# Linear attention into a gated MLP, batch 0: k loaded ahead of q, beta under the loads, kv evacuated from two banks by DVE and ACT

## The chip, the cores and the metric

One Trainium2 chip, one of its cores. The metric is the device time of one launch in microseconds (us); several runs are taken and the median is quoted. A profile is one execution; its span (first to last instruction) is some 2 us shorter than the time of the same run (300.0 against 301.74 us in the kernel before). TensorE (PE), VectorE (DVE), ScalarE (ACT) and GpSimd (POOL) run side by side (busy for 287.4, 123.9, 176.1 and 52.0 of the 300.0 us of the kernel before); POOL issues nearly all of the loads here, into one queue (q0 of the page, 20.45 MB, 47.1% of the time of 16 DMA engines); only beta's 8 KB go by SyncE.

## The reference, cut to what matters

```python
batch, n_heads, seq, head_dim = (8, 8, 576, 64)
phi = lambda x: np.where(x > 0, x, np.exp(x) - 1.0) + 1.0
q_p, k_p = (phi(q), phi(k))
kv  = np.einsum('bhsd,bhse->bhde', k_p, v)
z   = np.sum(k_p, axis=2)
num = np.einsum('bhsd,bhde->bhse', q_p, kv)
den = np.einsum('bhsd,bhd->bhs', q_p, z)[..., None] + 1e-06
x   = (num / den)            # 4608 tokens x 512
h   = x @ w_in               # 512 x 2048
g   = h * (1.0 / (1.0 + np.exp(-beta * h)))
out = g @ w_out              # 2048 x 512
```

## The kernel before

Batches run in a pipeline: the attention of batch b+1 is done under the h and y matmuls of batch b (y is g @ w_out). Batch 0 has nothing to hide under, so its loads and its attention are the start of the program. It uses a layout of nine tokens per partition: partitions 0 to 63 hold heads 0 to 3 (g = 0), partitions 64 to 127 heads 4 to 7 (g = 1).

```python
    load_nine(q9, q, j1=4)          # the queue's order: q's first 4 of 9 tokens
    load_nine(k9, k)
    make_identity(nc, identity)
    make_identity(nc, ident16)
    load_nine(v9, v, h1=2)
    load_nine(v9, v, h0=2)
    load_nine(q9, q, j0=4)
    for i in range(4):
        nc.gpsimd.dma_start(out=w_in_sb[i], in_=w_in_v[:, :, i * 512 : (i + 1) * 512])
    load_w_out(0)
    load_w_out(1)
    load_k(1)                       # k and q of batch 1
    load_q(1)
    # ... cut ...
    warm(WARM)                      # 20 matmuls on zeros
    beta_trans()
    # ... cut ...
    exp0(0, 0, 4)                   # 0 is q, 1 is k
    relu0(0, 0, 4)
    phi0(0, 0, 4)
    exp0(1, 0, 5)
    exp0(1, 5, N9)
    qb = att_banks(BF16)
    q_trans0(0, qb, 0)
    q_trans0(1, qb, 256)
    warm(8)
    q_out0(0, qb, 0, False)
    q_out0(1, qb, 256, False)
    relu0(1, 0, 5)
    relu0(1, 5, N9)
    phi0(1, 0, 5)
    phi0(1, 5, N9)
    v_copy0(0, 2)
    make_beta()                     # five small DVE operations
    kvp = att_banks()               # one tile of two banks
    kv_mm0(0, kvp)                  # 18 matmuls
    warm(2)
    v_copy0(2, HH)
    kv_mm0(1, kvp)                  # 18 matmuls
    kv_evac0(kvp)                   # two DVE copies of 64 x 260
    warm(3)
    num_mm(0, 0)
    num_mm(0, 1)
    # ... cut: exp of q's rest, table load for Silu, num_norm, x_trans, then h_phase(0) ...
    h_last(0, xT[0], [F(exp_, 1, 1), F(exp_, 1, 0), F(w_out_scale, 2, dve=False)])
```

`warm` is there to keep TensorE's clock from falling (before_warm and kq1_less_warm below test it: with more of these matmuls the granted clock from 12.3 to 15.7 us was 1.00 for 0.51, with fewer 0.51 for 1.00). `h_last` is the end of batch 0's h phase; the exps of batch 1's k and q follow it on ACT.

## Time and profile before

| | before |
|---|---|
| median of 4 runs (301.73 to 302.92) | 302.12 us |
| profiled span | 300.0 us |
| exp of k starts | 10.12 us |
| first h matmul of batch 0 | 20.73 us |
| ACT's table load for the exps of batch 1 | 35.69 us |

### The profile page before, as it was taken

What the parts mean: (1) busy time and instruction counts of PE and PEld (TensorE: products, weight loads), DVE (VectorE), ACT (ScalarE), POOL (GpSimd) and SP (SyncE); (2) the same over time, 40 slices, a digit from 0 to 9 for tenths busy, and PEclk for the clock granted to TensorE, in tenths of its full rate; (3) what the DMA queues carried; (4) which work ended last, traced back from release to release, by engine and by line L of the source; (5) the groups of instructions that cost most, each with busy time, mean ns of one, the idle gap of its engine ahead of it and who ended that gap; (6) DMA issues with size and microseconds to landing.
All of it is one profiled execution on the core that took longest, in us unless ns stands there. A gap on an engine that the chain in (4) does not pass through costs nothing.

```text
span 300.0 us, 4706 instructions
## 1 busy us (share of the span) xinstructions
PE 287.4 (96%) x1877; PEld 146.1 (49%) x1898; DVE 123.9 (41%) x248; ACT 176.1 (59%) x232; POOL 52.0 (17%) x72
## 2 busy tenths in 40 slices
PE   8599998999999999999999999999999999999994
PEld 3257545654556444445444544454445444444444
DVE  4567495801476145714571457144714400110012
ACT  3448896789988791579157915691661067007600
POOL 8834466432202300060002000000000000000000
PEclk9879999999999999999999999999999999999999
DMA  6999999999917974399538165125412510010033
GB/s 80 195 207 341 248 278 192 213 234 181 161 40 192 164 124 123 97 155 173 129 94 111 53 98 130 29 56 130 98 26 57 127 37 0 35 72 35 0 71 71
DMA packets 69206, 36.43 MB, mean 121 GB/s; under 512 B 37808, under 2 KB 63680, under 8 KB 69184
## 3 DMA queue, kind: packets, MB, share of 16 engines
q0 software_dynamic: 38400, 20.45, 47.1%
q1 hardware_dynamic: 30624, 15.55, 20.5%
q8 instruction: 15, 0.25, 0.3%
q10 hardware_dynamic: 160, 0.13, 0.2%
q14 instruction: 7, 0.06, 0.1%
HBM read 36.71 MB, written 9.44 MB: 154 GB/s over the span
## 4 chain that ended last, share of the span: by engine, by line
PE 81%; ACT 7%; DMA 4%; issue 3%; DVE 2%; POOL 1%; ACTq 0%; POOLq 0%
PE mm L443 39%; PE mm L495 33%; PE att L389 3%; ACT e L225 3%; DMA xqk<-in_k_dram 2%; DMA xqk<-in_q_dram 2%; PE att L335 2%; PE mm L527 1%; PE mm L562 1%; ACT q_pT L362 1%; ACT w_out L210 1%; ACT L225 1%; PE att L301 1%; ACT e L252 1%; POOL xqk L133 1%
## 5 line engine op out<-in xcount | busy, mean ns | idle before, releaser
L435 ACT ACTIVATE g<-mm,beta_c 128x512 bf16<-128x512 f32 (+2 forms) x156 | 97.4, 632 | 92.3 <-PE mm L443 91.9
L495 PE MATMUL mm<-w_out,g 128*128 128x512 bf16 x541 | 127.4, 379 | 1.2 <-issue 0.3
L443 PE MATMUL mm<-xT,w_in 128*128 128x512 bf16 (+2 forms) x560 | 107.8, 349 | 0.8 <-DVE xT L360 0.8
L443 PEld LDWEIGHTS <-w_in 128*128 128x128 bf16 x656 | 62.2, 98 | 61.7 <-issue 1.0
L495 PEld LDWEIGHTS <-g 128*128 128x128 bf16 x560 | 52.7, 97 | 57.1
L505 DVE COPY y_sb<-mm 128x512 f32<-128x512 f32 x27 | 18.7, 692 | 70.4 <-PE mm L495 68.4
L225 ACT ACTIVATE e<-xqk 128x2560 bf16<-128x2560 bf16 x14 | 31.9, 2329 | 0.1
L405 DVE TENSOR_TENSOR xs<-att,rden 128x512 bf16<-128x512 f32 (+1 forms) x40 | 27.6, 690 | 1.6 <-DVE rden L404 0.2
L238 DVE TENSOR_TENSOR qk_p<-r,e 128x2560 bf16<-128x2560 bf16 x14 | 20.9, 1490 | 14.6 <-ACT e L225 13.9
L345 DVE CAST kv_bd<-att 64x260 bf16<-64x260 f32 x14 | 6.0, 427 | 36.8 <-PE att L335 36.7
L73 POOL DMA_DIRECT2D vraw<-in_v_dram x7 | 6.2, 881 | 77.0 <-DVE vaug L360 71.0
L403 DVE TENSOR_SCALAR den<-att 128x8 f32<-128x8 f32 (+1 forms) x40 | 6.5, 161 | 29.1 <-PE att L389 29.1
L389 PEld LDWEIGHTS <-q_pT 128*128 128x128 bf16 (+1 forms) x160 | 12.2, 103 | 10.9 <-DVE xs L405 2.1
L389 PE MATMUL att<-kv_bd,q_pT 128*128 128x130 bf16 (+1 forms) x160 | 16.4, 227 | 0.8 <-ACT q_pT L362 0.5
L443 PE MATMUL mm<-xT_tail,w_in 128*128 128x512 bf16 x63 | 13.9, 379 | 0.1
L233 DVE TENSOR_SCALAR r<-xqk 128x2560 bf16<-128x2560 bf16 x14 | 11.6, 836 | 4.4 <-DMA xqk<-in_q_dram 2.2
L562 PE MATMUL mm<-g 128*128 128x512 bf16 x36 | 11.8, 483 | 1.6 <-DVE g L145 1.2
L73 POOL DMA_DIRECT2D xqk<-in_k_dram x7 | 7.0, 1005 | 15.6 <-ACT e L225 8.5
L252 ACT ACTIVATE e<-xqk 128x1024 bf16<-128x1024 bf16 (+1 forms) x4 | 4.5, 1159 | 8.2 <-DMA xqk<-in_q_dram 4.3
L225 ACT ACT_TABLE_LOAD x7 | 9.0, 1283 | 0.1
L73 POOL DMA_DIRECT2D xqk<-in_q_dram x7 | 7.7, 1102 | 5.9 <-DMA w_in<-in_moe_w_in_dram 1.9
L404 DVE RECIPROCAL rden<-den 128x8 f32<-128x8 f32 (+1 forms) x40 | 8.1, 201 | 1.4
(72 smaller groups left out, 144.9 us busy)
## 6 DMA issues: line engine op xcount, KB each, us to landing
out_dram<-y_sb SPq DMA_DIRECT2D x28, 256.0 KB, 2.3
xqk<-in_k_dram POOLq DMA_DIRECT2D x7, 512.0 KB, 10.7
xqk<-in_q_dram POOLq DMA_DIRECT2D x7, 512.0 KB, 11.6
vraw<-in_v_dram POOLq DMA_DIRECT2D x7, 512.0 KB, 12.3
w_in<-in_moe_w_in_dram POOLq DMA_DIRECT2D x4, 512.0 KB, 10.2
g<-in_moe_w_out_dram POOLq DMA_DIRECT2D x4, 512.0 KB, 11.1
out_dram<-y_sb SPq DMA_DIRECT2D x14, 128.0 KB, 5.2
xqk<-in_moe_w_out_dram POOLq DMA_DIRECT2D x2, 512.0 KB, 13.9
```

The source lines that it names most:

```text
L73: eng.dma_start(out=dst[:, :, 0:NJ, :].rearrange("p h j d -> p h (j d)"), in_=src[b, :, 0:MAIN, :].rearrange("h (p j) d -> p h (j d)", j=NJ),)
L225: nc.scalar.activation(st[b, "e", a][:, h0:h1], xqk[b % NX][:, a, h0:h1], ACTF.Exp)
L233: nc.vector.tensor_scalar(st[b, "r", a][:, h0:h1], xqk[b % NX][:, a, h0:h1], 0.0, 1.0, ALU.max, ALU.add)
L238: nc.vector.tensor_tensor(st[b, "p"][:, a].rearrange("p j (h d) -> p h j d", h=H)[:, h0:h1], st[b, "r", a][:, h0:h1], st[b, "e", a][:, h0: ...
L389: nc.tensor.matmul(nps[:n, p // 2, c0 : c0 + 2 * (D + 1)], st[b, "qT"][:, t, p, :n], kv_bd[b % 2][:, p], start=True, stop=True, skip_group ...
L404: nc.vector.reciprocal(rden[:n], den[:n])
L405: nc.vector.tensor_mul(xs[:n], nv[:, :, :, 0:D], rden[:n, :, :, None].to_broadcast([n, 2, 4, D]))
L435: nc.scalar.activation(g_sb[b % 2][:, ff, c0:c1], hp[:, c0:c1], ACTF.Silu, scale=beta_c[:, ff : ff + 1],)
L443: nc.tensor.matmul(hp[:, c0:c1], w_in_sb[ff // 4][:, kc, (ff % 4) * P : (ff % 4 + 1) * P], x[:, t0:t1, kc, :] if b < B else x[:, kc, c0:c1 ...
L495: nc.tensor.matmul(yp, g_sb[b % 2][:, ff, t * P : (t + 1) * P], w_out_sb[ff // 4][:, ff % 4, :], start=(ff == 0), stop=(ff == FC - 1),)
L505: nc.vector.tensor_copy(y_sb, yp)
L562: nc.tensor.matmul(st["warm"], g_sb[0][:, FC - 1, 0:P], g_sb[0][:, FC - 1, :], start=True, stop=True, skip_group_check=True,)
```

## The change

Its intent: k is needed before q, so it is loaded first; beta needs only DVE and a small transpose, so it is done while the loads run; the two head halves, which already lie in two banks of one tile, get a tile each, and the evacuation is split by bank, so that DVE empties one while ACT empties the other. The core of the diff:

```diff
+    load_nine(k9, k)
     load_nine(q9, q, j1=4)
-    load_nine(k9, k)
@@ kv_evac0, kv_bd split in two tiles by head half g
-        for i in range(2):
-            copy(kv_bd[0][gs, :, i, :]..., kvp[gs, :, ...], True)
+        for g in range(2):
+            for i in range(2):
+                copy(kv_bd[0][g][gs, :, i, :], kvp[g][gs, ...], g == 0)
@@ the start of batch 0 (cut)
-    warm(WARM)
+    warm(10)
     beta_trans()
-    exp0(0, 0, 4)  relu0(0, 0, 4)  phi0(0, 0, 4)
-    exp0(1, 0, 5)  exp0(1, 5, N9)
+    make_beta()
+    warm(20)
+    exp0(1, 0, 5)  exp0(1, 5, N9)  exp0(0, 0, 4)
+    relu0(1, 0, 5) relu0(1, 5, N9) phi0(1, 0, 5)
+    relu0(0, 0, 4) phi0(1, 5, N9)  phi0(0, 0, 4)
+    v_copy0(0, 2)
     q_trans0(0, qb, 0)
     q_trans0(1, qb, 256)
-    warm(8)
+    kvp = [mm_bank([P, 512]) for _ in range(2)]
+    kv_mm0(0, kvp)
     q_out0(0, qb, 0, False)
     q_out0(1, qb, 256, False)
-    # ... k's relu and phi, v_copy0(0, 2), make_beta, kv_mm0(0), warm(2) ...
+    warm(1)
     v_copy0(2, HH)
     kv_mm0(1, kvp)
     kv_evac0(kvp)
-    warm(3)
+    warm(1)
@@ plan of the h phase
-            3: [F(x_trans, 0, 1, dve=True), ...
+            3: [F(x_trans, 0, 1), ...
```

Because kv_bd is split, the later batches evacuate kv with four DVE copies of 64 x 130 in place of two of 64 x 260.

More of the change, by code (lines that the diff above doesn't have):

```diff
@@ L41 @@
     DMA_T = 3
-    WARM = 20
     TINY = 2.0 ** -30
@@ L165 @@
     load_q(1)
-    kv_bd = [consts.tile([P, KC, 2, D + 1], BF16, name=f"kv_bd{i}") for i in range(2)]
+    kv_bd = [
+        [consts.tile([P, 2, 2, D + 1], BF16, name=f"kv_bd{i}{g}") for g in range(2)]
+        for i in range(2)
+    ]
     for i in range(2):
-        nc.vector.memset(kv_bd[i], 0.0)
+        for g in range(2):
+            nc.vector.memset(kv_bd[i][g], 0.0)
     def set_ones(i):
@@ L301, in kv_mm0 @@
                 nc.tensor.matmul(
-                    kvp[:, g, m0 : m0 + 2 * (D + 1)],
+                    kvp[g][:, m0 : m0 + 2 * (D + 1)],
                     st["p0"][1][gs, j, 2 * a : 2 * a + 2, :],
@@ L308, in kv_evac0 @@
     def kv_evac0(kvp):
-        for i in range(2):
-            gs = slice(i * D, (i + 1) * D)
-            copy(
-                kv_bd[0][gs, :, i, :].rearrange("p (g a) e -> p g a e", g=2),
-                kvp[gs, :, 0 : 4 * (D + 1)].rearrange(
-                    "p g (a i e) -> p g a i e", a=2, i=2
-                )[:, :, :, i, :],
-                True,
-            )
+        for g in range(2):
+            for i in range(2):
+                gs = slice(i * D, (i + 1) * D)
+                copy(
+                    kv_bd[0][g][gs, :, i, :],
+                    kvp[g][gs, 0 : 4 * (D + 1)].rearrange(
+                        "p (a i e) -> p a i e", a=2, i=2
+                    )[:, :, i, :],
+                    g == 0,
+                )
     def v_copy(b, h0=0, h1=H, dve=True):
@@ L340, in kv_mm, with kv_evac @@
                     )
-    def kv_evac(b, p0=0, p1=KC):
-        for g in range(2):
-            gs = slice(g * D, (g + 1) * D)
-            nc.vector.tensor_copy(
-                kv_bd[b % 2][gs, p0:p1, g, :], st[b, "kvp"][gs, p0:p1, :]
-            )
+    def kv_evac(b):
+        for i in range(2):
+            for g in range(2):
+                gs = slice(g * D, (g + 1) * D)
+                nc.vector.tensor_copy(
+                    kv_bd[b % 2][i][gs, :, g, :], st[b, "kvp"][gs, 2 * i : 2 * i + 2, :]
+                )
     def rows(t):
@@ L391, in num_mm @@
                 st[b, "qT"][:, t, p, :n],
-                kv_bd[b % 2][:, p],
+                kv_bd[b % 2][p // 2][:, p % 2],
                 start=True, stop=True, skip_group_check=True,
@@ L580 @@
     ]
-    exp0(0, 0, 4)
-    relu0(0, 0, 4)
-    phi0(0, 0, 4)
     exp0(1, 0, 5)
     exp0(1, 5, N9)
+    exp0(0, 0, 4)
+    relu0(1, 0, 5)
+    relu0(1, 5, N9)
+    phi0(1, 0, 5)
+    relu0(0, 0, 4)
+    phi0(1, 5, N9)
+    phi0(0, 0, 4)
+    v_copy0(0, 2)
     qb = att_banks(BF16)
@@ L588 @@
     q_trans0(1, qb, 256)
-    warm(8)
+    kvp = [mm_bank([P, 512]) for _ in range(2)]
+    kv_mm0(0, kvp)
     q_out0(0, qb, 0, False)
     q_out0(1, qb, 256, False)
-    relu0(1, 0, 5)
-    relu0(1, 5, N9)
-    phi0(1, 0, 5)
-    phi0(1, 5, N9)
-    v_copy0(0, 2)
-    make_beta()
-    kvp = att_banks()
-    kv_mm0(0, kvp)
-    warm(2)
+    warm(1)
     v_copy0(2, HH)
@@ L603 @@
     kv_evac0(kvp)
-    warm(3)
+    st["warm"] = mm_bank([P, 512])
+    warm(1)
     num_mm(0, 0)
@@ L644 @@
             1: [F(q_second)],
-            3: [F(x_trans, 0, 1, dve=True), F(num_mm, 0, 2), F(num_norm, 0, 2)],
+            3: [F(x_trans, 0, 1), F(num_mm, 0, 2), F(num_norm, 0, 2)],
             5: [F(num_mm, 0, 3), F(num_norm, 0, 3)],
```

## The prediction

Terms of the split evacuation were only the author's estimate: the sum gives it 0.65 us with its gaps (15.3 to 15.95), where the kernel before took 0.87 on DVE (two casts of 64x260 at 428 ns). With them the sum came to the first h matmul at 18.6 against 20.73, 2.1 us earlier; less 0.27 for xT that is the 1.8, and with 1.7 the time of 300.8. Cut are the terms of which the unchanged 10.7 is made up, a term of DVE for the later evacuations that the sum does not count, and, of the third rival, how the clock would fall before h and its price (time about 302).

> **What bounds the kernel now.** The page's shares come first: TensorE is busy in nearly all 40 slices, except that the granted clock is low in one early slice and DVE and ACT carry the first slices. The change touches only batch 0 and (in two small places) the later batches, so I then read the chain of waits for the first 60 us, piece by piece, and the timeline and the windows beside it.
>
> From the page of the kernel before, the 40 slices (7.5 us each):
> ```profile
> PE   8599998999999999999999999999999999999994
> PEclk9879999999999999999999999999999999999999
> DMA  6999999999917974399538165125412510010033
> ```
> In slices 0 to 2 TensorE is not the limit: it is partly idle or slowly clocked, and much of its work there is warm-up. From about 20 us on it is. DMA is full until about 82 us, so I must ask whether an earlier start only runs into later loads.
>
> From the chain in order of time (start us, us, what):
> ```profile
> 3.20 6.84 DMA xqk<-in_k_dram
> 10.12 2.23 ACT e L252 x2
> 12.98 0.47 DVE vaug L292
> 13.49 1.16 PE att L301 x18
> 14.98 0.63 PE mm L562
> 15.62 1.09 PE att L301 x17
> 16.70 1.39 PE mm L562 x3
> 18.10 0.87 PE att L389 x8
> 20.25 0.42 DVE xT L360
> ```
> The start is a serial chain: k lands at 10.04, exp, v copy, two kv groups of 18 matmuls, evacuation, num, normalise, transpose, copy, and the first h matmul at 20.73 (timeline). **From k's landing to the first h matmul are 10.69 us.** Two pieces are not needed work: the stretch from 14.65 to 15.54 between the kv groups, and the three warm-up matmuls that hold num back until 18.10.
>
> From the timeline (start us, us, engine line op, tile, form, count, idle before):
> ```profile
> 5.17 1.06 ACT L252 ACTIVATE e<-xqk 128x1024 bf16<-128x1024 bf16 x1 [2.93 <-DMA xqk<-in_q_dram]
> 10.12 2.22 ACT L252 ACTIVATE e<-xqk 128x1280 bf16<-128x1280 bf16 x2 [3.90 <-DMA xqk<-in_k_dram]
> 14.18 0.25 DVE L201 RECIPROCAL rbeta<-beta_c 128x16 f32<-128x16 f32 x1
> 14.35 0.40 DVE L292 COPY vaug<-vraw 128x1152 bf16<-128x1152 bf16 x1
> 16.75 0.87 DVE L360 CAST kv_bd<-att 64x260 bf16<-64x260 f32 x2 [2.00 <-PE att L301]
> ```
> q is used early (5.17), but nothing on the path needs it; ACT then waits 3.90 us for k. The five small beta operations (13.35 to 14.35) stand on DVE between the two v copies, so the second v copy, and with it the second kv group, is late. The evacuation takes 0.87 on DVE alone.
>
> [...] The windows of this trace show clock 1.00 to 12.4, 0.50 from 12.4 to 18, and 1.00 from 20. It drops after TensorE had nothing from 10.15 to 12.30.[...]
>
> **The change part by part.**
>
> *k ahead of q.* All of these loads go through one queue, and landings follow the cumulated bytes. The windows by half microseconds show 40, 86, 185, 189 GB/s from 2.5 to 4.5 (q's two transfers, 128 KB each), then a new ramp of 57, 67, 108, 131, 136, 177, 198, 175, 180 to 9.0, in which k's 576 KB (two of 288 KB) pass; it lands 1.05 later. Two estimates for k first: the same ramp 1.9 us earlier gives 8.15; q's ramp, then about 185 GB/s, gives 250 KB by 4.5 and the other 340 (in thousand bytes, 590 in all) by 6.35, landing at 7.4. I choose **7.9** for k. q's first part then comes at about 9.3 to 10, the sum of both being unchanged. So k gains 2.1 us.
>
> *The path after it.* In the new order DVE does the phi of k, then that of q's first half, then the v copy; so ACT's exp of q (1.06) and DVE's phi of q (0.69) are now on the path, which they were not. In its place beta (0.95 us of DVE) is done under the loads, and of the two and the three warm-up matmuls one each remains.
> - exp of k: 7.9 + 0.08 + 2.22 = 10.2; exp of q 1.06: 11.26; phi of q 0.69: 11.98 with gaps; v copy 0.46: 12.46
> - kv group one 1.16: 13.65; one warm-up at low clock 0.43: 14.1; group two 1.16: 15.3. The second v copy needs v's second part, which by the cumulated bytes lands at about 13.1, before 14.1.
> - evacuation: [...] 15.95. The one warm-up lies within it, where three used to end at 18.10.
> - num to first den 0.47 (18.10 to 18.57 before): 16.45; den, reciprocal, xs 1.13: 17.6; transpose, copy, start of h 1.03: **18.6 against 20.73**, 2.1 us earlier.
>
> The path from k's landing is thus as long as before (10.7): beta, warm-ups and half an evacuation go[...], q's exp and phi come (1.75). **The gain is k's earlier landing.**
>
> *xT of tile 1 by ACT.* At 22.94 DVE copied it in 0.42, and the next h group began at 23.42. On ACT it stands behind the activations that end at 23.03 and takes 0.60: 23.63, 0.27 later. DVE is freed for the next normalisation, but TensorE sets the pace just after. I charge 0.27.
>
> *kv_evac of later batches*: four copies of 130 in place of two of 260[...]. In batch 1 the cast ends at 48.36 and num starts at 50.89, waiting for ACT; in batch 2 DVE has gaps of 0.55 after it; from batch 3 on several us lie between. No time.
>
> Sum: 2.1 − 0.27 = **about 1.8 us**; I take 1.7 for joints.
>
> **Does the gain survive?** TensorE bounds most of the rest, so an earlier start would carry through, if no load stops it. Limits from the trace: w_in's first part had landed when the POOL queue went on at 17.48 (h starts at 18.6); k of batch 1 at 33.54 and its q at 36.82 (DVE was waiting for each), used by ACT at 36.98 and 39.22, so the q leaves 2.4 us; w_out's third part by about 38.8 (the queue moved on), used at 41.45, leaves 2.7. v of batch 1 lands at 42.04, used at 42.42: only 0.4, but what follows on DVE (copy 1.12, phi 1.47) is needed by TensorE at 46.63 and 48.42, so it has about 2 us. A gain of 1.8 just fits; one over 2.4 would be cut there.
>
> **Rivals.**
> - *The queue gives nothing back*: k's ramp belongs to the first bytes of k, and k lands only at 8.8 or later. The low rates of 5.5 to 7.0 speak for it, q's 185 GB/s against. Then q's exp and phi on the path eat most of it: gain 0.5 to 0.9, time about 301.8.
> - *ACT becomes the bound*: exp of k, exp of q, two q copies, two evacuations, exp of q's rest, table load, all before the first Silu. My count: evacuation ends 15.95, exp 1.27, table load 1.28, dummy 0.2: 18.7, and the first Silu needs h at about 19.1. It just fits. If an evacuation waits behind the q copies, a few tenths are lost.
> - *The clock*: [...] For it: two warm-ups fewer. Against: the kv groups now follow each other more closely[...].
> - *Hidden anyway*: loads of batch 1 or ACT's stretch from 35 to 46.6 (exps, w_out scaling) absorb it: same time. The slack above speaks against.
>
> **Range and chances.** 302.49 − 1.7 = 300.8. The runs of before spread over 1.2 us, k's landing is uncertain by 0.5 us, and the clock by up to 1; this gives 299.7 to 302.1. 2% would be 6 us, more than half of the whole start; nothing in the change is worth that either way. Faster by over 2%: 0.01; within 2%: 0.98; slower: 0.01.
>
> **What would show it.** k's exp starting at about 8 (step 1; later than 8.8 makes me wrong); beta's operations before it; q's exp right behind without a wait; both kv groups 0.5 us apart or less; DVE and ACT evacuating side by side in under 0.7; the first h matmul at 18.3 to 19; the first exp of batch 1 about 1.8 earlier than 36.98, and the same shift near 100 us. If the shift at h is there and is gone by 50 us, the fourth rival is right; if the clock row is low between 19 and 23, the third.

## More of the kernel before

Of the timeline of the kernel before, the columns are start us, us, engine, line, operation, tiles, form, count, and in brackets the idle time just before and what ended it.

```profile
20.73 0.61 PE L443 MATMUL mm<-xT,w_in 128*128 128x128 bf16 x8 [0.52 <-DVE xT L360]
35.69 1.28 ACT L225 ACT_TABLE_LOAD   x1
```

The second has no bracket: ACT had finished the Silu in front of it at 35.67, and nothing held it.

## The result, and the profile after

302.12 us before (4 runs, 301.73 to 302.92), **299.07 us** after (4 runs, 298.99 to 299.32). The ratio is 0.9897, with a 95% interval of 0.9873 to 0.9922. Ratios and intervals here and below are those of the fast runs of the same rounds, so not quite the ratio of the medians quoted.

The slices of the changed kernel, to be laid beside those of before in the prediction:

```profile
PE   8789978999999999999999999999999999999994
PEclk9999999999999999999999999999999999999999
DMA  7999999999928954599457255024502400020032
```

The row to look at is the clock: the 8 and the 7 of slices 1 and 2 (counted from 0) are gone. (The prediction speaks of one low slice; its own row shows two.) TensorE is a little less busy in slice 2 than before, 8 tenths for 9, and yet not slowed.

The timeline of the changed kernel, same columns:

```profile
6.92 3.16 ACT L255 ACTIVATE e<-xqk 128x1280 bf16<-128x1280 bf16 x3 [4.68 <-DMA xqk<-in_k_dram]
11.24 0.69 PE L304 MATMUL mm<-vaug,qk_p 64*128 64x130 bf16 x18
11.90 0.58 DVE L295 COPY vaug<-vraw 128x1152 bf16<-128x1152 bf16 x1 [0.72 <-DMA vraw<-in_v_dram]
12.54 0.69 PE L304 MATMUL mm<-vaug,qk_p 64*128 64x130 bf16 x18 [0.60 <-DVE vaug L295]
13.25 0.60 DVE L365 CAST kv_bd<-mm 64x130 bf16<-64x130 f32 x2 [0.77 <-PE mm L304]
13.28 0.56 ACT L367 ACTIVATE kv_bd<-mm 64x130 bf16<-64x130 f32 x2 [0.88 <-PE mm L304]
16.50 0.61 PE L448 MATMUL mm<-xT,w_in 128*128 128x128 bf16 x8 [0.52 <-DVE xT L365]
...
33.05 1.28 ACT L228 ACT_TABLE_LOAD   x1 [1.49 <-DMA xqk<-in_k_dram]
```

The three exps (two of k, one of q) run back to back from 6.92. A kv group takes 0.69 us where it took 1.16. DVE and ACT empty the banks side by side (0.60 and 0.56). The first h matmul is at 16.50. And the last line is new in kind: ACT's table load now waits 1.49 us for a load, that of k of batch 1, which it did not wait for before. The second v copy too now waits for its load, since beta no longer stands in front of it.

How the shift runs through the program, from the two timelines:

| point | before | changed | earlier by |
|---|---|---|---|
| exp of k starts | 10.12 | 6.92 | 3.20 |
| first h matmul | 20.73 | 16.50 | 4.23 |
| last Silu before the exps of batch 1 ends | 35.67 | 31.56 | 4.11 |
| table load for those exps starts | 35.69 | 33.05 | 2.64 |
| kv of batch 1 evacuated from | 47.49 | 44.84 | 2.65 |
| kv of batch 7 evacuated from | 222.95 | 220.22 | 2.73 |
| end of the span | 300.0 | 297.2 | 2.8 |

So there are three things to explain: why k was a whole microsecond earlier than foreseen, where another microsecond up to h came from, and where 1.5 us were lost between 31.56 and 33.05. The chain of waits of the changed kernel (start us, us, what) shows the last of them:

```profile
4.74 2.35 POOL vraw L132 x4
7.09 1.24 POOL xqk L132 x2
8.32 0.67 POOL w_in L160
8.99 10.71 DMA w_in<-in_moe_w_in_dram
19.99 12.99 DMA xqk<-in_k_dram
33.05 1.28 ACT L228
34.34 1.94 ACT e L228
```

Up to 33 us the chain no longer passes through batch 0's arithmetic at all. It is the load queue: POOL issues, w_in lands and lets the queue go on (POOL waited 2.74 us for it before the issue at 19.99), k of batch 1 is issued and lands, and then comes the table load. Whatever batch 0 gains beyond this is not seen in the end.

### The profile page after: what moved, and what is told of

It is laid out like the page before. It is cut to its first block, busy times and chain, and to the rows that moved or that the text cites. A ratio compares the mean times of both kernels' runs of the same rounds, so it can differ in the third digit from the quotient of the medians.

```text
span 297.2 us, 4721 instructions
## 1 busy us (share of the span) xinstructions
PE 284.8 (96%) x1876; PEld 144.6 (49%) x1897; DVE 125.0 (42%) x263; ACT 177.2 (60%) x235; POOL 52.1 (18%) x72
## 4 chain that ended last, share of the span: by engine, by line
PE 71%; DMA 17%; ACT 6%; POOL 3%; issue 2%; DVE 0%; POOLq 0%; ACTq 0%
PE mm L448 33%; PE mm L500 32%; DMA xqk<-in_q_dram 5%; DMA xqk<-in_k_dram 4%; DMA vraw<-in_v_dram 4%; DMA w_in<-in_moe_w_in_dram 4%; PE att L394 2%; ACT e L228 2%; PE att L339 2%; POOL xqk L132 1%; PE mm L532 1%; ACT g L440 1%; ACT L228 1%; ACT w_out L213 1%; POOL vraw L132 1%
## 5 line engine op out<-in xcount | busy, mean ns | idle before, releaser
L350 DVE CAST kv_bd<-att 64x130 bf16<-64x130 f32 x28 | 8.2, 292 | 35.0 <-PE att L339 34.7
L394 PE MATMUL att<-kv_bd,q_pT 128*128 128x130 bf16 (+1 forms) x160 | 15.8, 221 | 1.1 <-ACT q_pT L367 0.4
L567 PE MATMUL mm<-g 128*128 128x512 bf16 x35 | 10.0, 440 | 1.2 <-DVE g L144 1.2
L72 POOL DMA_DIRECT2D xqk<-in_k_dram x7 | 6.2, 891 | 12.8 <-ACT e L228 6.5
L76 POOL DMA_DIRECT2D xqk<-in_k_dram x7 | 7.6, 1082 | 2.7 <-DMA w_in<-in_moe_w_in_dram 2.7
## 6 DMA issues: line engine op xcount, KB each, us to landing
xqk<-in_k_dram POOLq DMA_DIRECT2D x7, 512.0 KB, 10.7
```

The costliest lines, as they stand in the source:

```text
L72: eng.dma_start(out=dst[:, :, 0:NJ, :].rearrange("p h j d -> p h (j d)"), in_=src[b, :, 0:MAIN, :].rearrange("h (p j) d -> p h (j d)", j=NJ),)
L350: nc.vector.tensor_copy(kv_bd[b % 2][i][gs, :, g, :], st[b, "kvp"][gs, 2 * i : 2 * i + 2, :])
L394: nc.tensor.matmul(nps[:n, p // 2, c0 : c0 + 2 * (D + 1)], st[b, "qT"][:, t, p, :n], kv_bd[b % 2][p // 2][:, p % 2], start=True, stop=True ...
L567: nc.tensor.matmul(st["warm"], g_sb[0][:, FC - 1, 0:P], g_sb[0][:, FC - 1, :], start=True, stop=True, skip_group_check=True,)
```

## The experiments

**The theory** after the first look: the gain at h is the sum of k's earlier landing (3.2 us) and of the clock that stays full (about 1.1 us), while the small parts (beta, evacuation, xT by ACT) weigh little; and all beyond 2.65 us is cut by the landing of batch 1's k. **Rivals:** the load order is nothing and the new order of work with the clock carries it; the small parts carry it; ACT's chain or w_out's scaling, not k's load, makes the cut.

### q loaded first again (label q_first)

```diff
-    load_nine(k9, k)
     load_nine(q9, q, j1=4)
+    load_nine(k9, k)
```

> The changed kernel with q's first part loaded ahead of k again, all else as changed. Theory (k's earlier landing is most of the gain): exp of k starts at about 10.1 us in place of 6.92, the first h matmul comes 3 us or more later (19.5 or later, from 16.50), the gain left is under 1.2 us: time 301.0 to 302.3. Rival (the order of the work and the full clock carry the gain, the load order is nothing): time within 0.5 of 299.1.

Measured: 302.61 us against 301.96 of before in the same rounds, ratio 1.0027 (0.9999 to 1.0056). The exps of k start at 10.30, the first h matmul at 20.97. **Without the load order nothing of the change's gain is left**; it was even a little more than I expected to lose. The clock fell as well, in this windows view (stretch, length, busy time of PE, PEld, DVE, ACT and POOL with counts, granted clock, DMA share, GB/s):

```profile
12.30:15.70 3.40, 1.27 (x34) 1.18 (x34) 2.71 (x6) 2.17 (x4) 3.40 (x5) 0.83 1.29 204
15.70:19.10 3.40, 2.74 (x35) 1.80 (x32) 1.33 (x5) 1.46 (x4) 1.20 (x2) 0.67 1.24 205
```

In the kernel before the clock fell earlier, at 12.3 for 14.5 here, and stayed low for longer:

```profile
12.30:15.70 3.40, 1.88 (x23) 1.28 (x26) 2.24 (x8) 2.03 (x4) 3.40 (x5) 0.51 1.29 203
15.70:19.10 3.40, 3.40 (x30) 2.13 (x27) 1.81 (x6) 1.73 (x3) 1.16 (x2) 0.50 1.24 206
```

In the changed kernel both stretches have clock 1.00. So this run mixes two causes: k is late, and because it is late TensorE idles from 9.6 to 14.25 and is slowed. They had to be told apart.

### The clock, in the kernel before (label before_warm)

```diff
-    warm(8)
+    warm(20)
     q_out0(0, qb, 0, False)
```

> The kernel before with 20 in place of 8 warm-up matmuls behind the first q transposes, nothing else. Theory (full clock through the kv and num stage is worth about 1.5 us at h): clock 1.00 from 12.4 to 19, each kv group of 18 matmuls about 0.7 us in place of 1.16, first h matmul at 18.7 to 19.5 in place of 20.73, time about 300.6 (300.0 to 301.2). Rival (DVE's beta operations and v copies set the pace there, clock or not): first h matmul after 20.2, time within 0.5 of before.

Measured: 300.55 us, ratio 0.9951 (0.9924 to 0.9977), as expected. The clock is 1.00 throughout, the kv groups take 0.69 us, the first h matmul is at 18.51, a little before my range. Part of that is chance: the profiled run is the fastest of the four (299.51), and in it k came 0.6 us early (exp at 9.49). From the exp of k to h it takes 9.02 us, against 10.61 before: 1.59 us for the clock. Twelve matmuls on zeros bought about half of the change's gain.

### The clock, with q first (labels q_first_warm, q_first_warm34)

```diff
     make_beta()
-    warm(20)
+    warm(40)      # q_first_warm; 34 in q_first_warm34
```
on top of q_first.

> q_first (the changed kernel, q's part loaded first) with 40 in place of 20 warm-up matmuls behind the beta transpose, so that the clock stays full though k is late. Theory (k's landing and the clock add up: about 3 us and about 1.5 us at h): clock 1.00 throughout, first h matmul at 19.0 to 19.9 (20.97 in q_first, 16.50 with k first), time 300.2 to 301.4. Rival (all of the gain is the clock, which the late k only lets fall): first h matmul before 18, time under 299.6.

Measured: 301.46 us, ratio 0.9985. The clock was 1.00, but the edit spoiled its own result: the 40 matmuls ended at 15.28 and held the q transposes until 15.20, though the phi of q that they need had ended at 14.41 (the expectation below says 14.2, too early). First h matmul 20.36, out of the range I gave. So again with 34:

> q_first_warm mended: its 40 warm-up matmuls ended at 15.28 and held the q transposes (ready at 14.2) back to 15.20; 34 end at about 13.5. Theory (k's landing is worth about 3 us at h, the clock about 1 to 1.5 beside it): clock 1.00, q transposes at about 14.2 without a hold, first h matmul at 19.2 to 19.9 against 20.97 in q_first and 16.50 with k first, time 300.3 to 301.1. Rival (the clock carries the most): first h matmul before 18.5.

Measured: 301.25 us, ratio 0.9969 (0.9948 to 0.9991). The hold is gone and the clock is full, but in the profiled execution k landed late (exp at 10.90), so h came at 20.35, again outside my range; the time missed it by little. What counts is the distance from the exp of k to h: 9.45 us, against 10.67 in q_first.

### The clock, with k first (label kq1_less_warm)

On top of kq1_early (below), which has no cut by batch 1's k, so that a loss at h is seen in the time:

```diff
     make_beta()
-    warm(20)
```

> kq1_early without the 20 warm-up matmuls behind the beta transpose. Theory (they keep the clock full through the kv and num stage, worth about 1 us or more): clock 0.50 in at least 10.9 to 15, kv groups about 1.16 us each in place of 0.69, first h matmul at 17.4 to 18.8, time 0.9 to 2 us over kq1_again. Rival (the clock stays full, or the stage waits on DVE and loads anyway): within 0.3 of kq1_again.

Measured: 298.89 us, against 297.88 of the same kernel with the 20 matmuls in the same rounds (kq1_again): 1.0 us slower. The windows view:

```profile
8.90:12.30 3.40, 0.99 (x24) 0.88 (x26) 3.16 (x6) 1.97 (x3) 3.40 (x6) 0.50 1.21 190
12.30:15.70 3.40, 3.26 (x39) 1.94 (x35) 1.19 (x4) 1.59 (x5) 2.31 (x3) 0.51 1.26 206
```

Half clock from 8.8 to 15.6, kv groups of 1.16 us, first h matmul at 18.01. These runs together:

| run | loaded first | clock from 12.3 to 15.7 | exp of k | first h | between |
|---|---|---|---|---|---|
| before | q | 0.51 | 10.12 | 20.73 | 10.61 |
| before_warm | q | 1.00 | 9.49 | 18.51 | 9.02 |
| q_first | q | 0.83 (0.67 after) | 10.30 | 20.97 | 10.67 |
| q_first_warm34 | q | 1.00 | 10.90 | 20.35 | 9.45 |
| changed | k | 1.00 | 6.92 | 16.50 | 9.58 |
| kq1_less_warm | k | 0.51 | 7.32 | 18.01 | 10.69 |

In the new order of work the stretch from the exp of k to h is 10.7 us at low clock and 9.5 at full clock, whichever load comes first. **So the clock is worth 1.1 to 1.2 us, and the load order the rest: 3.2 us.** They add. In the old order of work the clock is worth more, 1.6 us (before against before_warm). Each row is one execution.

The granted clock for every execution, averaged over the program, shows the same cost inside one kernel. At half clock the profiles spend either 3.4 us (14.54 to 17.95 in q_first) or twice that (12.34 to 19.16 in before), worked out from the granted clock of the stretches with 0.50 as the low one; the means of the program are 0.994 and 0.987. The executions of the kernel before in the experiments fall into two groups to match: 23 with a clock of 0.991 to 0.994 take 301.5 us on average, 17 with 0.986 to 0.988 take 302.3. The groups overlap, and the profiled execution is of the second, costlier kind, so the clock's share of the median gain is less sure than its 1.1 us in the profiles. One thing does not fit: the only execution of kq1_less_warm that kept its clock (0.999) was its slowest, 299.38 us. No trace of it is kept.

### The load order alone (label order_alone)

The same edit as the first lines of the diff, in the kernel before, with the engines still taking q's work first.

> The kernel before with k loaded ahead of q and nothing else: the engines still take q's work first. Theory (the early k pays only with k's work put first): exp of q starts at about 8.3, those of k behind it at about 9.4 in place of 10.12; first h matmul 0.3 to 1.2 us earlier than 20.73, time 0.2 to 1.2 us under before. Rival (the load order alone carries the gain): first h matmul at 18 or earlier, time under 300.

Measured: 299.91 us, ratio 0.9940 (0.9921 to 0.9959), more than I expected: by its time the run falls to the rival, by the first h matmul, at 19.13 and 1.6 us earlier, to neither. But this is not k's landing: ACT waits for q until 9.01, and the exps of k follow at about 10.05 (9.01 + 1.04), as late as in the kernel before. From there to h are 9.1 us, the 9.02 of before_warm. The clock stayed at 1.00, most likely because the eight warm-up matmuls behind the q transposes now ran from 11.19 to 13.09, just ahead of the kv groups. So here the load order paid by accident, through the clock: the one execution of six that lost it (0.993) took 300.88 us, the other five 299.77 to 300.14. An early k alone does not bring k's work forward; that work must come first as well.

### The small parts (labels small_back, kq1_small_back)

```diff
-                    g == 0,
+                    True,                  # both halves evacuated by DVE
     beta_trans()
-    make_beta()
     warm(20)
     v_copy0(0, 2)
+    make_beta()
-            3: [F(x_trans, 0, 1), ...
+            3: [F(x_trans, 0, 1, dve=True), ...
```

> The changed kernel with three parts undone: the beta operations back behind the first v copy, both halves of the evacuation on DVE, xT of tile 1 copied by DVE. Theory (the gain at h is larger than what the loads of batch 1 let through, 1.5 us lie in the wait for k of batch 1): the first h matmul comes 0.3 to 1.2 us later than 16.50, but the exps of batch 1 still start at about 34.3, time 299.0 to 299.5. Rival (these parts are on the path that sets the end): time later by what h loses, 299.7 to 300.4.

Measured: 298.95 us, ratio 0.9905 (0.9883 to 0.9927), as the changed kernel. The first h matmul came at 17.22, 0.7 later, and none of it is in the time, since ACT still waited for k of batch 1:

```profile
32.73 1.28 ACT L228 ACT_TABLE_LOAD   x1 [0.59 <-DMA xqk<-in_k_dram]
```

The wait shrank from 1.49 to 0.59 and took up the loss. To see the parts, the cut had to go first. With kq1_early below:

> kq1_early with the same three parts undone as in small_back (beta back, evacuation by DVE alone, xT of tile 1 by DVE). Theory (they were worth 0.7 us at the first h matmul and 0.6 at the end of batch 0's h phase, hidden behind the wait for k of batch 1; with that wait gone they show): 0.4 to 0.8 us slower than kq1_again. Rival (they are worth nothing anywhere): within 0.2.

Measured: 298.14 against 297.88, 0.26 us slower, between the theory and the rival, and the runs of the two overlap (298.05 to 299.20 against 297.75 to 298.24). The profiled spans are 296.4 and 295.9, and the table load came at 32.16 in place of 31.64, although k's exp had started 0.21 earlier (6.69 against 6.90): from the exp to the table load it is 0.73 us longer. So the three parts together are worth some tenths, 0.3 in the times and up to 0.7 along the path, and nothing in the changed kernel as it stands. What each is worth alone was not tested.

### The cut: batch 1's loads earlier (labels kq1_early, after_again, kq1_again, before_kq1_early)

```diff
     load_w_out(0)
-    load_w_out(1)
     load_k(1)
     load_q(1)
+    load_w_out(1)
```

> The changed kernel with the loads of k and q of batch 1 issued ahead of w_out's second part in place of behind it. Theory (k of batch 1, landing at 33.03, cuts the gain at h from 4.2 to 2.65 us): k lands at about 30.4, the table load for the exps follows the last Silu at 31.6 without a wait, time about 297.8 (297.4 to 298.3). Rival (ACT's chain or w_out's scaling cuts it at the same place): time within 0.4 of 299.1.

Measured: 298.16 us, ratio 0.9879 (0.9855 to 0.9903). The wait is gone; table load and exps in the timeline of kq1_early:

```profile
31.70 1.28 ACT L228 ACT_TABLE_LOAD   x1
33.00 4.57 ACT L228 ACTIVATE e<-xqk 128x2560 bf16<-128x2560 bf16 x2
```

k of batch 1 lands at 29.8, ahead of its use; from here on the program runs 1.3 us ahead of the changed kernel. As the intervals of the two ratios overlap, both kernels were timed again in the same rounds:

> The changed kernel itself, timed in the rounds of the three below so that they can be compared: 299.1, with the table load of batch 1's exps waiting about 1.5 us (0.6 to 1.5) for k of batch 1.

> The same kernel as kq1_early, timed again beside the changed one. Theory (the load of k of batch 1 cuts the changed kernel's gain): 0.7 to 1.4 us below it, about 298.0. Rival (the earlier difference was noise between jobs): within 0.3 of it.

Measured: 298.98 us for the changed kernel (ratio 0.9911, 0.9892 to 0.9929; its table load waited 1.57 us) and 297.88 us for kq1_early (0.9876, 0.9857 to 0.9895; six runs of 297.75 to 298.24, none as slow as the fastest of the changed kernel, 298.65). **1.1 us more, from moving one line**: this version beats both kernels. In after_again the h matmuls themselves waited 0.54 us for w_in's first part, so batch 0 is close to its own load limit as well.

The control, the same move in the kernel before:

> The kernel before with the same move of batch 1's k and q loads ahead of w_out's second part. Theory (these loads cut only where the start is early; in the kernel before k of batch 1 lands at 33.5, ahead of its use behind the table load at 35.69): within 0.4 us of before. Rival (the loads of batch 1 bind the kernel before too): 0.7 to 1.4 us faster than before, as in the changed kernel.

Measured: 301.59 against 301.64, ratio 0.9992 (0.9973 to 1.0010). Nothing: the load of batch 1's k binds only where batch 0 is early. The wait was made by the change.

## Why the prediction was wrong

The direction and the absence of a 2% effect held, and the mechanism "The gain is k's earlier landing" held for the larger part, 3.2 of the 4.2 us at the first h matmul. The size did not: 299.07 lies below the range's 299.7, and the gain is 3.05 us (2.6 in the rounds of after_again) where I had 1.7. By its steps:

- **"I choose 7.9 for k": the term was mis-sized.** "So k gains 2.1 us" measured 3.2: the exp starts at 6.92. Over all profiles it starts between 6.56 and 7.32 with k first (order_alone aside, where it stands behind q's), and between 9.49 and 10.90 with q first, so the difference is beyond the scatter. The windows by half microseconds (the last two columns are DMA share and GB/s) show it; of the kernel before, k behind q:

```profile
4.50:5.00 0.50, 0.50 (x2) 0.15 (x1) 0.00 (x0) 0.00 (x0) 0.45 (x2) 1.00 0.69 57
5.00:5.50 0.50, 0.50 (x3) 0.18 (x2) 0.32 (x1) 0.33 (x1) 0.50 (x2) 1.00 0.92 67
5.50:6.00 0.50, 0.50 (x4) 0.26 (x3) 0.11 (x1) 0.50 (x1) 0.50 (x2) 1.00 0.93 108
```

  and of the changed kernel, k first:

```profile
2.50:3.00 0.50, 0.50 (x3) 0.23 (x2) 0.50 (x2) 0.00 (x0) 0.50 (x2) 1.00 0.55 39
3.00:3.50 0.50, 0.50 (x3) 0.21 (x2) 0.47 (x4) 0.00 (x0) 0.50 (x2) 1.00 0.88 118
3.50:4.00 0.50, 0.50 (x3) 0.15 (x1) 0.07 (x1) 0.00 (x0) 0.50 (x2) 1.00 1.23 212
4.00:4.50 0.50, 0.50 (x2) 0.15 (x1) 0.00 (x0) 0.00 (x0) 0.41 (x3) 1.00 1.14 191
```

  k first is near 200 GB/s a microsecond after its start. The thin stretch of before, where the share falls to 0.69, is not a property of k's transfers, as my first estimate (8.15) had it, but of the second place: q's transfers behind k's in the changed kernel dip as well (186, then 128 GB/s at 6.0). The dip differs between executions: k behind q ran at 57, 67 and 108 in before, but at 127, 131 and 173 in before_warm. My second estimate (7.4) had the right idea; I took a value between the two, and even the second was cautious. Why the queue runs thin there, no run shows.

- **"kv group one 1.16", "one warm-up at low clock 0.43": the step that failed outright.** I carried the low clock of before into the changed kernel. It stayed at 1.00, and the kv groups took 0.69 each. Before, TensorE had no matmul from 10.15 to 13.49 (the 12.30 of the prediction is a lone weight load); in the changed kernel the warm-up matmuls end at 9.91 and the q transposes start at 10.87. Without the 20 warm-up matmuls it falls although k is early (kq1_less_warm, 0.50 and 0.51), and with them it falls when k is late (q_first, 0.83 and 0.67). I had named the chance that the new order wins full clock earlier and left it out of the sum. From the exp of k to h it made 1.1 us: 9.58 in the changed kernel. At low clock the same stretch takes 10.67 and 10.69 us in q_first and kq1_less_warm: the "10.7" of the prediction was right for the clock it assumed.

- **The small terms.** The evacuation took 0.60 us on DVE and 0.56 on ACT, side by side, for the 0.65 that the sum gave it with its gaps. xT by ACT cost 0.17 for the 0.27 charged (the shift is 4.23 at the first h matmul and 4.06 at the matmuls that wait for this xT, 23.42 and 19.36). The longer evacuation of the later batches (1.21 to 1.23 us for four copies, 0.87 for two) cost nothing: the shift stays at 2.65 to 2.73 from batch 1 to batch 7.

- **"Does the gain survive?": right to ask, wrong on the wait that ends last.** I gave batch 1's q 2.4 us and its k 3.4 (33.54 against the exp at 36.98). But the exp's table load stands in front of it (1.28 us; in before 1.31 from the end of the Silu, 35.67, to the start of the exp) and waits for k as well (1.49 us in the changed kernel), so k had only 35.69 − 33.54 = 2.15 us. k landed half a microsecond earlier in the changed kernel (33.03), which makes 2.64. A gain of 4.11 us came to this place and 2.64 passed. That my limit of 2.4 lies near is luck: it came from q. kq1_early shows the cause, before_kq1_early that it is new.

In one sum: 1.8 foreseen, plus 1.1 for k, 1.1 for the clock and 0.1 from the small terms makes 4.1 at the end of the h phase; minus 1.5 at batch 1's k leaves 2.6. The two large errors pointed the same way, and the cut took back only part.

Of the rivals, the clock was the right thing to look at, with the sign reversed; the queue "giving nothing back" and ACT as the bound before h are refuted (ACT's dummy Silu ends at 16.65, the first Silu starts at 16.92 waiting for TensorE); "hidden anyway" is true for over a third of the gain at h.

What stays open: why the transfers in second place run thin, why k's landing scatters by over a microsecond between executions of kernels with the same loads up to there, and when exactly the clock falls. The length of TensorE's gap alone does not decide it: in before_kq1_early the granted clock fell (0.76 from 12.3 to 15.7, 0.74 from there to 19.1) after a gap of 2.64 us (11.00 to 13.63, the first line), while order_alone kept 1.00 through one of 2.80 us (8.05 to 10.85, the second):

```profile
13.63 0.83 PE L301 MATMUL att<-vaug,qk_p 64*128 64x130 bf16 x18 [2.64 <-DVE vaug L292]
10.85 0.41 PE L278 MATMUL att<-identity,qk_p 64*128 64x64 bf16 x16 [2.80 <-DVE qk_p L266]
```

By the same reckoning as above the low stretches lasted 3.4 us (q_first and before_kq1_early) or twice that, 6.8 (before and kq1_less_warm); what sets their length, no run shows.

## What to carry to other kernels

When work is moved towards an earlier time in a chain with warm-up matmuls, ask whether an idle gap of TensorE opens or closes: here the clock was worth as much as a third of the loads' gain, and twelve matmuls on zeros in the old kernel had half of the whole gain. Before counting a gain to the end, follow the load queue for the next thing that lands just in time, and count a table load that stands in front of its user (here 1.28 us). A part that is "worth nothing" in the time may lie behind such a wait, so test it again with the wait removed.
